# An adaLN block with 32 heads on one core: zero matmuls, GpSimd fills, the table load and the tie-break seeds of a list scheduler

## The chip, the cores and the metric

The kernel runs on 1 core of one Trainium2 chip. The metric is the device time of one execution in microseconds (us). The program is written for five engines with queues of their own: TensorE (PE), VectorE (DVE), ScalarE (ACT), GpSimd (POOL) and SyncE (SP), which issues nearly all DMAs.

## The reference

One transformer block of 2048 rows, width 512, 32 heads of 16, hidden width 1376, in bf16. The vector `c` gives six modulation rows through `w_mod`.

```python
mod = (_silu(c) @ w_mod).reshape(c.shape[0], 6, 1, -1)
sa, ca, ga, sb, cb, gb = (mod[:, 0], mod[:, 1], ..., mod[:, 5])
h = _layernorm(x) * (1 + ca) + sa
x = x + ga * _A_ref(h, A_wqkv, A_wo)                  # softmax attention, 32 heads
h = _layernorm(x) * (1 + cb) + sb
x = x + gb * _B_ref(h, B_w1, B_b1, B_w2, B_b2)        # gelu(h @ w1 + b1) @ w2 + b2
```

## The kernel before, in words

**Tiling.** The 2048 rows are four blocks of 512 (four tiles of 128 each). Attention goes by runs: one run is one query block against all 16 key tiles for four heads, which sit in the four 32-row strips of TensorE. A score unit is one 128 x 512 tile of scores of one head. Two engines take the exponentials from PSUM. ACT takes units two and three at a time and applies Exp (line 1082). DVE takes single units, adds a constant and writes int16, which are read as bf16 powers of two (line 1123); four shifted copies of each such tile (lines 1139, 1155, and on GpSimd 1161), multiplied with values scaled by four weights (the VX tiles, line 961), make the approximation smooth. TensorE computes scores (line 1034), then the products with the values, accumulated in the bank `od` (line 1222).

**The order of work.** Nothing is ordered by hand. At build time a list scheduler, `Plan`, simulates the five engines with a guessed duration for each `Op`. At each step `pick` looks, for each engine, at the operations that could start within a small slack of the first one, and takes the one with the least priority. To this `spread` (line 164) adds up to 0.15, a hash of the planned time (in slices of 12.5 us, each with its own entry of `SEEDS`) and, for operations that aren't PE's, of the line number of the operation's lambda. So the seeds and the line numbers settle ties and near ties. The guessed durations set only the order; on the chip the engines wait on semaphores.

**Keeping TensorE's clock up.** `commit` (line 214) keeps a list of what PE did. If less than HEAT = 1.5 us of array work lies within the last WIN = 3.4 us of planned time, `heat` (line 482) supplies a matmul by the zero tile `warm`: into a free `ax` bank, into the free `od` bank, or, while a run accumulates, as four adds of zero into `od` (`zeros`, line 500). Score products that go to `od` are doubled by zeros in the same way (line 1226).

**One-column sums.** The modulation rows needed as columns, `modB` (sb and cb), are 8 columns of 4 one-column matmuls each (`mod_mm`, line 656). Behind every second column there stands a zero matmul of 384 columns.

**The front.** The first 25 us load x, `w_mod` and the weights, normalise block 0 (`first_norm`) and make its keys, queries and values; exponentials begin, while blocks 1 to 3 are normalised (`parted_norm`; the rows are scaled by `apply`, line 703). GpSimd fills the parts of the value tiles and of the query tiles `qm` that must hold constants (`v_init` 617, `fill` 625, `o_qz` 903). These fills may be planned before 4.6 us or after block 0 is normalised (`early`, line 632; those of `qm` only after). GpSimd also computes the reciprocal root of each norm (`rstd`, line 695). Operations with `port=True` are planned so that DVE's and GpSimd's don't overlap; the fills aren't marked so, the `apply` are. `fits` asks if DVE's next marked operation leaves room; `after_dve` makes a GpSimd instruction wait for the last DVE instruction but one that was issued up to then.

**The end.** Block 3 is handled in two halves. For its last two query tiles the runs are short; `last_tile` (tile 2) and `last_last` (tile 3) project, normalise and run the MLP while the MLP of tiles 0 and 1 (`block_tail` with nt = 2) fills in. Its Gelus wait until all scores are done (`finished`), so ACT loads the Gelu table once, ahead of the first of them in ACT's order. There are two kinds: four pieces for tiles 0 and 1 (line 1476, of which the first is charged 1.3 us for the load), and one over tile 2 (line 1569, charged 1.2 us).

Of the kernel before, what the change touches and what calls it, by code (L numbers as in the profile page):

```python
# [11 lines left out]
ACT = mybir.ActivationFunctionType  # L12
# [38 lines left out]


WIN = 3.4
PEL = 0.24
PEA = 0.38
OVER = 0.0
# [4 lines left out]
AL = 0.055  # L61
FILL = 1.6
SPREAD = 0.15
SEEDS = (118, 698, 446, 86, 892, 273, 31, 57, 754, 651, 382, 787, 223, 128, 602, 744, 188, 333, 922, 439, 126, 575, 750, 516, 486, 576, 568, 332, 464, 494, 369, 909, 695, 214, 876, 486, 865, 254, 984, 347, 648, 207, 351, 794, 757, 475, 181, 40, 889, 834, 265, 449, 537, 182, 641, 600, 63, 147, 391, 720, 850, 728, 549, 401)
HEAT = 1.5
STRETCH = 12.5

# [41 lines left out]
class Plan:  # L109
# [104 lines left out]
    def commit(self, s, o):  # L214
        self.lists[o.eng].remove(o)
        self.now = s
        if o.acq is not None:
            o.slot = min(range(len(o.acq.free)), key=lambda i: o.acq.free[i])
            o.acq.free[o.slot] = 1e18
            o.tile = o.acq.alloc(o.slot)  # L220
        if o.kind == "pv" and s >= self.cool and o.last_left() > 1:
            o.extra, o.us = True, 2 * o.us
        if o.rows is not None:
            o.row = min(o.rows, key=lambda i: self.tiles.get(i, 0.0) if self.mode == "qk" else i)
            o.mode = ("qk", o.row)
        if o.eng == "PE":
            self.done.append((s, o.hot * (o.us if o.mode[0] != "qk" else o.us * (len(o.mode) - 1) / 4)))
            while self.done[0][0] < s - 30.0:
                self.done.popleft()
            tot = 0.0  # L230
            self.fill_at = self.cool = 0.0
            for t, us in reversed(self.done):
                tot += us
                if tot >= HEAT and not self.cool:
                    self.cool = t + WIN
                if tot >= self.fill:
                    self.fill_at = t + WIN
                    break
            if o.mode[0] != self.mode:
                self.mode, self.tiles = o.mode[0], {}  # L240
            for i in o.mode[1:]:
                self.tiles[i] = s + o.us
            self.free["PE"] = s + 0.01
        else:
            self.free[o.eng] = s + o.us
            if o.port:
                self.port[o.eng] = s + o.us
            if o.eng == "DVE" and o.us > 0:
                self.dve = (s, s + o.us, o.port)
# [38 lines left out]
def kernel(  # L288
# [14 lines left out]
    nc = tc.nc  # L303
# [4 lines left out]
    NC = D // P  # L308
# [173 lines left out]
    def heat():  # L482
        if o_warm.end is None or plan.now > plan.until:
            return None
        if min(r_ax.free) <= max(plan.now, plan.cool) and (n_a[0] > 0 or r_od.free[0] > plan.now):
            return Op("PE", lambda o: nc.tensor.matmul(
                out=o.tile, lhsT=warm, rhs=warm[:, 0:1].to_broadcast([P, QB]), start=True, stop=True),
                MM, (o_warm,), lat=PEL, mode=("full", 0), kind="heat", acq=r_ax)
        r = pv_run[0]
        if r is None and r_od.free[0] <= plan.now:  # L490
            return Op("PE", lambda o: nc.tensor.matmul(
                out=o.tile, lhsT=warm, rhs=warm[:, 0:1].to_broadcast([P, QB]), start=True, stop=True),
                MM, (o_warm,), lat=PEL, mode=("full", 0), kind="heat", acq=r_od)
        if r is None or left[r] == 0:
            return None
        return Op("PE", lambda o: zeros(r), MM, (o_warm,), lat=PEL, mode=("pv", 0), kind="heat")

    pv_run = [None]

# [114 lines left out]

    o_v0 = {}

    def v_init(v, w, prio, gate):
        x = v[..., 0:32 * VW].rearrange("p t (h w) -> p t h w", w=VW)
        return [op("POOL", lambda o, to=to, c=c: fill(to, c), 0.2, prio=prio, gate=gate)
                for to, c in ((v[..., 32 * VW:32 * VW + 15], 0.0), (x[:, :, 8:32:8, 0:15], 0.0), (x[..., 16:17], w))]  # L620

    first_ln = [False]
# [1 line left out]

    def fill(to, c):
        got = nc.gpsimd.memset(to, c)
        if first_ln[0] and not filled[0]:
            filled[0] = True
            tc.add_manual_dep(got.ins, z_end[0].ins.name, mybir.DependencyInfo(
                mybir.DependencyClass.Sync, mybir.DependencyReason.DATA), reason="behind the first norm")  # L630

    def early():
        return plan.now < EARLY or first_ln[0]
    o_vx0 = {}
    for b in range(NQ):
        o_v0[b] = v_init(VEB[b], PH_W[0], 1.0 + b, early)
        for t in DKS:
            if t // TPB == b:
                o_vx0[t] = [x for ph in range(1, NPH) for x in v_init(
                    VX[(t, ph)].unsqueeze(1), PH_W[ph], 1.5 + b, early)]  # L640

    o_ce = op("ACT", lambda o: nc.scalar.activation(out=ce, in_=c_bf, func=ACT.Tanh, scale=0.5),
              0.5, (o_c,), prio=0.0)
# [12 lines left out]
    def mod_mm(ps, n, w, m, warmer):  # L656
        col = ps[:, n * NC + m:n * NC + m + 1]
        for j in range(NC):
            nc.tensor.matmul(out=col, lhsT=w[:, j, m * P:(m + 1) * P], rhs=sc[:, j:j + 1],
                             start=(j == 0), stop=(j == NC - 1))  # L660
        if m % 2 and warmer:
            nc.tensor.matmul(out=ps[:, P:QB], lhsT=warm, start=True, stop=True,
                             rhs=warm[:, 0:1].to_broadcast([P, QB - P]))

    def mod_columns(dst, ws, kind, warmer=True):
        mm = chain([(lambda ps, n=n, w=w, m=m: mod_mm(ps, n, w[1](), m, warmer), 0.36 if warmer else 0.22)
                    for n, w in enumerate(ws) for m in range(NC)],
                   [o_sc, o_warm, ws[0][0]], kind, r_ax, [w[2] for w in ws],
                   need=lambda i: ws[i // NC][0], hot=(0.0, 0.45) if warmer else (0.0,))

        def out_(o):
            nc.vector.tensor_copy(out=dst, in_=mm.tile[:, 0:2 * NC])
            nc.vector.tensor_scalar(out=dst[:, NC:2 * NC], in0=dst[:, NC:2 * NC], scalar1=1.0,
                                    scalar2=None, op0=ALU.add)
        return op("DVE", out_, 0.4, (mm,), prio=0.65, rel=(mm,))
# [222 lines left out]
    def make_k(b, cc, kind, acq, eng, after=None):  # L898
# [1 line left out]
        o_k[(cc, b)] = op(eng, lambda o: copy(eng, kT[cc][b], mm.tile[:, 0:QB]), 0.6 if eng == 'DVE' else 0.5, (mm,), prio=0.3,  # L900
                          rel=(mm,))

    o_qz = [op("POOL", lambda o, n=n, p=p: fill(QM[n][:, p, :], 0.0), 0.5, prio=0.5 + n, gate=lambda: first_ln[0])
            for n in range(1, 4) for p in range(2)]

    def make_q(b, cc, kind, acq):
# [519 lines left out]
    def evict_g(g, fs, lo, n, mm, prio=0.3):  # L1426
# [3 lines left out]
            in1=b1c[:, fs[0]:fs[0] + len(fs)].unsqueeze(2).to_broadcast([P, len(fs), n]), op=ALU.add),  # L1430
            0.07 + len(fs) * n * 0.00104, (mm, o_late["b1"]), prio=prio, rel=(mm,))

    def block_tail(b, nt=TPB):
        kind = "tail"
        due(prog() + 15, (TAIL if b < LAST - 1 else TAIL2 if b < LAST else TAIL3) / (9 * nt - 1))
# [39 lines left out]
        if part:  # L1475
            ge = [op("ACT", lambda o, lo=lo, hi=hi: nc.scalar.activation(
                out=g.tile[:, lo:hi, 0:N], in_=g.tile[:, lo:hi, 0:N], func=ACT.Gelu_apprx_tanh),
                0.2 * (hi - lo) * nt / 2 + 0.1 + 1.3 * (lo == 0), ev[lo:hi], lat=0.15, prio=0.5,
                gate=finished) for lo, hi in PARTS]
        else:  # L1480
            ge = [op("ACT", lambda o: nc.scalar.activation(  # L1481
# [58 lines left out]
    def last_tile(r):  # L1540
# [21 lines left out]
        for f0 in range(0, NF, 4):  # L1562
# [5 lines left out]
            ev.append(evict_g(g, fs, t * P, P, mm, 0.02))  # L1568
        ge = op("ACT", lambda o: nc.scalar.activation(  # L1569
            out=g.tile[:, :, t * P:(t + 1) * P], in_=g.tile[:, :, t * P:(t + 1) * P], func=ACT.Gelu_apprx_tanh),  # L1570
            1.2, ev, lat=0.15, prio=0.6, gate=finished)
        w2_part(t, ge, lambda f: ge, x2)

    def last_last(r, t, OT, x2):
# [11 lines left out]
               kind="last", prio=0.2)  # L1586
        st = op("DVE", lambda o: (stats(ln, t, acc.tile), plus_eps(nc.vector, ln, t, t + 1)), 1.0, (w, ln), prio=0.022)
        rs = op("POOL", lambda o: rstd(ln, t, t + 1, True), 0.8, (st,), prio=0.0)
        za = op("DVE", lambda o: apply(ln, z, t, acc.tile), 0.6, (rs, z), prio=0.021, rel=(acc,))
        xa = op("DVE", lambda o: nc.vector.tensor_copy(out=x2.tile[:, t, :], in_=acc.tile), 0.6, (w,), prio=0.2, rel=(acc,))  # L1590
        hd = []
        for e, js in (("DVE", (0, 1)), ("ACT", (2, 3))):
            def tr(o, js=js):
# [182 lines left out]
```

## Time and profile before

| what | value |
|---|---|
| timed runs | median 778.43 us of 3 (778.0 to 778.72) |
| the profiled execution | 777.17 us, span 775.4 us |
| busy share | PE 94%, DVE 94%, ACT 97%, POOL 32% |
| exponentials on ACT, line 1082 | 711.4 us, 626 instructions |
| score tiles on DVE, line 1123 | 314.1 us, 484 instructions |
| first exponential starts | 12.44 us |
| last exponential ends | 756.10 us |
| mean granted clock of TensorE | 0.993 |

The profile is one execution. In its groups, an instruction is named by line, engine, operation and tiles (out<-in), with a count, busy time and mean. An arrow in brackets tells which instruction ended an idle time ahead of it. In the stretches, the busy time of each engine is given with the number of instructions in brackets behind it, and PEclk is the clock that TensorE was granted (1.00 is full).

### The profile page before, as it was taken

How to read it: one execution, taken by the hardware profiler on the slowest of the kernel's cores; microseconds unless marked ns; L12 is line 12 of the kernel's file. 1: busy time of each engine (PE TensorE's matmuls, PEld its weight loads, DVE VectorE, ACT ScalarE, POOL GpSimd, SP SyncE). 2: the span in 40 equal slices, each digit the busy share in tenths (PEclk: the TensorE clock that was granted, in tenths of full speed). 3: DMA queues.
4: the chain of work that ended last, by engine and by line, in shares of the span. 5: the costliest groups of instructions: out<-in, count | busy, mean ns of one | idle time of the engine just before them, and what ended most of it. 6: DMA issues, size and time to landing. Idle time of an engine off the chain costs nothing.

```text
span 775.4 us, 22094 instructions
## 1 busy us (share of the span) xinstructions
PE 728.4 (94%) x8901; PEld 276.3 (36%) x8977; DVE 726.3 (94%) x1302; ACT 750.9 (97%) x675; POOL 248.4 (32%) x477
## 2 busy tenths in 40 slices
PE   8899999999999999999999999999999999999997
PEld 3433332333333222222222223232344434344554
DVE  8889988999999999999999999999899999979983
ACT  5999999999999999999999999999999999999994
POOL 7424531324434441232423233233114342202200
PEclk9999998999999999999999999999999999999999
DMA  7152010000021101000100000000111001100000
GB/s 218 41 168 57 20 42 21 22 17 12 17 74 25 28 22 48 18 9 21 43 19 23 29 24 13 22 20 26 33 53 28 17 19 46 26 22 20 22 4 28
DMA packets 34913, 27.51 MB, mean 35 GB/s; under 512 B 17826, under 2 KB 28675, under 8 KB 34811
## 3 DMA queue, kind: packets, MB, share of 16 engines
q1 hardware_dynamic: 34802, 26.10, 11.9%
q8 instruction: 70, 1.15, 0.6%
q14 instruction: 33, 0.26, 0.1%
q10 hardware_dynamic: 8, 0.00, 0.0%
HBM read 20.50 MB, written 2.59 MB: 30 GB/s over the span
## 4 chain that ended last, share of the span: by engine, by line
ACT 37%; PE 36%; DVE 16%; issue 11%; DMA 0%; DVEq 0%; ACTq 0%
ACT pt L1082 35%; PE od L1222 12%; PE st L1034 10%; DVE ph L1123 6%; DVE sh L1139 5%; PE ax L1399 3%; PE ax L1464 3%; PE ax L1034 2%; PE ax L875 2%; PE ax L946 1%; ACT g L1481 1%; DVE sh L1155 1%; PE ax L1393 1%; DVE ln_s L688 1%; DVE g L1471 1%
## 5 line engine op out<-in xcount | busy, mean ns | idle before, releaser
L1082 ACT ACTIVATE pt<-st 128x1536 bf16<-128x1536 f32 x626 | 711.4, 1313 | 6.4 <-PE st L1034 4.0
L1123 DVE TENSOR_SCALAR ph<-ax 128x512 int16<-128x512 f32 x484 | 314.1, 681 | 16.9 <-PE ax L1034 16.1
L1034 PE MATMUL st<-qm,kT 32*128 32x512 bf16 (+1 forms) x1664 | 246.7, 372 | 20.4 <-ACT pt L1082 14.8
L1139 DVE TENSOR_SCALAR sh<-ph 128x2048 int16<-128x2048 int16 x363 | 239.8, 696 | 3.0 <-PE od L1222 1.6
L1161 POOL TENSOR_TENSOR sh<-ph,pair_sh 128x256 int32<-128x256 int32 x209 | 128.0, 623 | 249.4 <-DVE sh L1139 169.3
L1222 PE MATMUL od<-sh,VX 128*32 128x512 bf16 (+2 forms) x2640 | 168.8, 327 | 3.5 <-DVE sh L1139 2.6
L1034 PE MATMUL ax<-qm,kT 32*128 32x512 bf16 (+1 forms) x512 | 164.6, 367 | 5.4 <-DVE ph L1123 3.9
L1034 PEld LDWEIGHTS <-kT 32*128 32x128 bf16 x2176 | 79.6, 91 | 238.1 <-issue 226.3
L1222 PE MATMUL od<-pt,VEB 128*32 128x512 bf16 (+2 forms) x2156 | 141.5, 324 | 0.2 <-ACT pt L1082 0.2
L1222 PEld LDWEIGHTS <-VX 128*32 128x32 bf16 x2640 | 61.1, 95 | 83.8 <-issue 72.6
L1222 PEld LDWEIGHTS <-VEB 128*32 128x32 bf16 x2816 | 65.4, 96 | 66.5 <-issue 52.1
L1291 POOL TENSOR_TENSOR OT<-OD,RB 128x256 bf16<-128x256 f32 x36 | 26.3, 741 | 84.4 <-DVE sh L1139 29.5
L1155 DVE TENSOR_SCALAR sh<-ph 128x2048 int16<-128x2048 int16 (+3 forms) x89 | 50.8, 578 | 1.1 <-PE od L1222 1.1
L1222 PE MATMUL od<-ph,VEB 128*32 128x512 bf16 (+2 forms) x660 | 48.8, 327 | 0.8 <-DVE OD L1264 0.7
L1464 PE MATMUL ax<-blk,W 128*128 128x512 bf16 (+1 forms) x153 | 40.9, 351 | 2.1 <-issue 1.1
L961 POOL TENSOR_SCALAR VX<-VEB 128x128 bf16<-128x128 bf16 x64 | 24.3, 380 | 37.4 <-DVE VEB L720 34.3
L1291 POOL TENSOR_TENSOR OS<-OD,RB 128x256 bf16<-128x256 f32 x24 | 17.2, 729 | 57.6 <-DVE sh L1139 29.3
L1399 PE MATMUL ax<-w,g 128*128 128x512 bf16 x108 | 30.2, 381 | 2.9 <-ACT g L1569 1.3
L875 PE MATMUL ax<-blk,w 128*128 128x512 bf16 x85 | 29.1, 391 | 2.0 <-issue 0.9
L699 POOL TENSOR_TENSOR rs<-rs,mhalf 128x2 f32<-128x2 f32 (+2 forms) x17 | 13.0, 762 | 40.9 <-DVE rs L693 40.0
L1471 DVE TENSOR_SCALAR g<-ax,b1c 128x512 bf16<-128x512 f32 x33 | 24.3, 742 | 0.5 <-PE ax L1464 0.4
L1399 PEld LDWEIGHTS <-g 128*128 128x128 bf16 x187 | 15.4, 97 | 24.1 <-issue 12.3
(133 smaller groups left out, 426.0 us busy)
## 6 DMA issues: line engine op xcount, KB each, us to landing
RB<-rn SPq DMA_DIRECT2D x120, 64.0 KB
xb<-in_A_x_dram SPq DMA_DIRECT2D x7, 512.0 KB
qm<-qs SPq DMA_DIRECT2D x120, 16.0 KB
out_dram<-o SPq DMA_DIRECT2D x15, 128.0 KB
W<-in_B_w_dram SPq DMA_DIRECT2D x1, 1376.0 KB
w<-in_A_wqkv_dram SPq DMA_DIRECT2D x3, 384.0 KB
g<-in_w_mod_dram SPq DMA_DIRECT2D x4, 256.0 KB
g<-in_w_mod_dram SPq DMA_DIRECT2D x2, 512.0 KB
```

Of the source, the lines that this page charges most:

```text
L875: return chain([(lambda ps, j=j: nc.tensor.matmul(out=ps[:, 0:QB], lhsT=w.tile[:, j, cc * P:(cc + 1) * P], rhs=o_h[b].tile[:, j, :], start ...
L1034: nc.tensor.matmul(out=o.tile[:, k * QB + n * w:k * QB + (n + 1) * w], lhsT=kT[cc][kb][rows, ko * P:(ko + 1) * P], rhs=qm.tile[rows, par, ...
L1082: nc.scalar.activation(out=e.tile[:, 0:len(got) * QB], in_=o.tile[:, 0:len(got) * QB], func=ACT.Exp, scale=ESC)
L1123: nc.vector.tensor_scalar(out=ph.tile[:, o.row * QB:(o.row + 1) * QB], in0=o.tile, scalar1=PH_B, scalar2=0.0, op0=ALU.add, op1=ALU.max)
L1139: sh = op("DVE", lambda o, j=j: nc.vector.tensor_scalar(out=o.tile, in0=first.tile, scalar1=PH_SH[j], scalar2=None, op0=ALU.add), 0.6, es, ...
L1155: return nc.vector.tensor_scalar(out=sh.tile[:, at], in0=first.tile[:, at], scalar1=PH_SH[-1], scalar2=None, op0=ALU.add)
L1161: return nc.gpsimd.tensor_tensor(out=sh.tile[:, at].bitcast(I32), in0=first.tile[:, at].bitcast(I32), in1=pair_sh[:, 0:1].to_broadcast([P, ...
L1222: nc.tensor.matmul(out=o_od[r].tile[32 * i:32 * i + 32, to:to + w], lhsT=v_tile(k, ph)[:, c0:c0 + 32], rhs=got[i][:, n * w:(n + 1) * w], s ...
L1291: two = beside(lambda c: nc.gpsimd.tensor_tensor(out=both_heads(OT.tile, tile_of[r]) if r in tile_of else OT.tile[:, c], in0=OD.tile[:, c] ...
L1399: nc.tensor.matmul(out=ps, lhsT=g[:, f, col:col + P], rhs=rhs[:, c], start=(f == 0), stop=(f == NF - 1))
L1464: mm = chain([(lambda ps, f=f, j=j, f0=f0: nc.tensor.matmul(out=ps[:, (f - f0) * N:(f - f0 + 1) * N], lhsT=W1[:, j, f * P:(f + 1) * P], rh ...
L1471: ev += [op("DVE", lambda o, f=f, f0=f0, mm=mm: nc.vector.tensor_scalar(out=g.tile[:, f, 0:N], in0=mm.tile[:, (f - f0) * N:(f - f0 + 1) * ...
```

## The change

Seven things, all in the code that makes the order or in single operations:

1. In the first 30 us of planned time, the window in which 1.5 us of array work must lie is 2.4 us, not 3.4.
2. `heat` prefers the adds of zero into `od` whenever a run accumulates; before, a free `ax` bank came first.
3. A zero matmul stands behind every one-column sum, not behind every second.
4. GpSimd's fills are marked `port`, with longer durations; after the first norm they are planned only where `fits` finds room, and each but the first waits for the DVE instruction before the last. Those of `qm` may also go before 4.6 us.
5. The load of the Gelu table is an ACT operation in the plan, without an instruction, ahead of both kinds of Gelu, whose durations are changed.
6. In `last_last`, the copy of the projected tile goes from DVE to ACT; the norm is planned behind it.
7. Nine of the 64 seeds differ, and the lines shift by 1 to 5.

```diff
+WIN_EARLY = 2.4
...
-SEEDS = (118, 698, ..., 651, 382, ..., 602, 744, 188, ..., 794, ..., 889, ..., 147, 391, 720, ...)
+SEEDS = (948, 698, ..., 651, 812, ..., 502, 744, 928, ..., 821, ..., 825, ..., 428, 944, 328, ...)
...
-            tot = 0.0
+            tot, win = 0.0, WIN if s > 30.0 else WIN_EARLY
...
-                    self.cool = t + WIN
+                    self.cool = t + win
...
-                    self.fill_at = t + WIN
+                    self.fill_at = t + win
...
     def heat():
         if o_warm.end is None or plan.now > plan.until:
             return None
+        if pv_run[0] is not None and left[pv_run[0]] > 0:
+            return Op("PE", lambda o, r=pv_run[0]: zeros(r), MM, (o_warm,), lat=PEL, mode=("pv", 0), kind="heat")
...
-        if r is None or left[r] == 0:
-            return None
-        return Op("PE", lambda o: zeros(r), MM, (o_warm,), lat=PEL, mode=("pv", 0), kind="heat")
+        return None
...
-    def v_init(v, w, prio, gate):
+    def v_init(v, w, prio, gate, us=0.25):
...
-        return [op("POOL", lambda o, to=to, c=c: fill(to, c), 0.2, prio=prio, gate=gate)
+        return [op("POOL", lambda o, to=to, c=c: fill(to, c), us, prio=prio, gate=gate, port=True)
...
-        if first_ln[0] and not filled[0]:
+        if first_ln[0] and filled[0]:
+            after_dve(got)
+        elif first_ln[0]:
...
-        return plan.now < EARLY or first_ln[0]
+        return plan.now < EARLY or first_ln[0] and plan.fits(0.3)
...
-                    VX[(t, ph)].unsqueeze(1), PH_W[ph], 1.5 + b, early)]
+                    VX[(t, ph)].unsqueeze(1), PH_W[ph], 1.5 + b, early, 0.13)]
...
-        if m % 2 and warmer:
+        if warmer:
...
-        mm = chain([(..., 0.36 if warmer else 0.22)
+        mm = chain([(..., 0.38 if warmer else 0.22)
...
-                   need=lambda i: ws[i // NC][0], hot=(0.0, 0.45) if warmer else (0.0,))
+                   need=lambda i: ws[i // NC][0], hot=(0.42,) if warmer else (0.0,))
...
-    o_qz = [op("POOL", ..., 0.5, prio=0.5 + n, gate=lambda: first_ln[0])
+    o_qz = [op("POOL", ..., 0.53, prio=0.5 + n, gate=early, port=True)
...
+    o_table = op("ACT", None, 1.3, (), lat=0.0, prio=-1.0, gate=finished)
...
-                0.2 * (hi - lo) * nt / 2 + 0.1 + 1.3 * (lo == 0), ev[lo:hi], lat=0.15, prio=0.5,
+                0.23 * (hi - lo) * nt / 2 + 0.05, ev[lo:hi] + [o_table], lat=0.15, prio=0.5,
...
-            1.2, ev, lat=0.15, prio=0.6, gate=finished)
+            1.4, ev + [o_table], lat=0.15, prio=0.6, gate=finished)
...
-        za = op("DVE", lambda o: apply(ln, z, t, acc.tile), 0.6, (rs, z), prio=0.021, rel=(acc,))
-        xa = op("DVE", lambda o: nc.vector.tensor_copy(out=x2.tile[:, t, :], in_=acc.tile), 0.6, (w,), prio=0.2, rel=(acc,))
+        xa = op("ACT", lambda o: nc.scalar.copy(out=x2.tile[:, t, :], in_=acc.tile), 0.62, (st,), prio=0.2, rel=(acc,))
+        za = op("DVE", lambda o: apply(ln, z, t, acc.tile), 0.6, (rs, z, xa), prio=0.021, rel=(acc,))
```

More of the change, by code (lines that the diff above doesn't have):

```diff
@@ L63 @@
 SPREAD = 0.15
-SEEDS = (118, 698, 446, 86, 892, 273, 31, 57, 754, 651, 382, 787, 223, 128, 602, 744, 188, 333, 922, 439, 126, 575, 750, 516, 486, 576, 568, 332, 464, 494, 369, 909, 695, 214, 876, 486, 865, 254, 984, 347, 648, 207, 351, 794, 757, 475, 181, 40, 889, 834, 265, 449, 537, 182, 641, 600, 63, 147, 391, 720, 850, 728, 549, 401)
+SEEDS = (948, 698, 446, 86, 892, 273, 31, 57, 754, 651, 812, 787, 223, 128, 502, 744, 928, 333, 922, 439, 126, 575, 750, 516, 486, 576, 568, 332, 464, 494, 369, 909, 695, 214, 876, 486, 865, 254, 984, 347, 648, 207, 351, 821, 757, 475, 181, 40, 825, 834, 265, 449, 537, 182, 641, 600, 63, 428, 944, 328, 850, 728, 549, 401)
 HEAT = 1.5
@@ L665, in mod_columns @@
     def mod_columns(dst, ws, kind, warmer=True):
-        mm = chain([(lambda ps, n=n, w=w, m=m: mod_mm(ps, n, w[1](), m, warmer), 0.36 if warmer else 0.22)
+        mm = chain([(lambda ps, n=n, w=w, m=m: mod_mm(ps, n, w[1](), m, warmer), 0.38 if warmer else 0.22)
                     for n, w in enumerate(ws) for m in range(NC)],
                    [o_sc, o_warm, ws[0][0]], kind, r_ax, [w[2] for w in ws],
-                   need=lambda i: ws[i // NC][0], hot=(0.0, 0.45) if warmer else (0.0,))
+                   need=lambda i: ws[i // NC][0], hot=(0.42,) if warmer else (0.0,))
         def out_(o):
@@ L901, in make_k @@
                           rel=(mm,))
-    o_qz = [op("POOL", lambda o, n=n, p=p: fill(QM[n][:, p, :], 0.0), 0.5, prio=0.5 + n, gate=lambda: first_ln[0])
+    o_qz = [op("POOL", lambda o, n=n, p=p: fill(QM[n][:, p, :], 0.0), 0.53, prio=0.5 + n, gate=early, port=True)
             for n in range(1, 4) for p in range(2)]
```

## The prediction

> **What bounds it now.** I read the engine table first: ScalarE (ACT) is 97% busy and 711.4 of its 750.9 us are the exponentials of line 1082. VectorE (DVE) and TensorE (PE) are both at 94%. All three matter, because planner lines 389 to 421 hand score tiles to ACT and to DVE as each comes free. The work has (34-2) x 16 x 4 = 2048 score units (TOTAL, line 979). Row L1123 shows DVE taking 484 of them, so ACT takes 1564. ACT needs 711.4/1564 = 0.455 us a unit. DVE needs (314.1+239.8+50.8)/484 = 1.25 us a unit. Together they finish 2.20 + 0.80 = 3.0 units a us. So a us of ACT idleness costs 0.73 us of the whole, and a us of DVE idleness 0.27 us. I use these two prices everywhere before the end.
>
> Next I read the busy table by stretches, to see where ACT and DVE are short. Columns: stretch, its length, busy us of PE, PE's weight loads, DVE, ACT, GpSimd (POOL), the granted clock, DMA share, GB/s.
>
> ```profile
> 12.44:25.20 12.76, 10.08 (x92) 4.72 (x93) 12.45 (x31) 10.77 (x13) 9.08 (x46) 0.87 0.45 146
> 25.20:116.00 90.80, 84.73 (x896) 32.56 (x900) 81.93 (x159) 90.75 (x87) 37.49 (x69) 1.00 0.23 63
> 116.00:122.80 6.80, 6.80 (x61) 2.02 (x61) 4.65 (x9) 5.56 (x5) 0.00 (x0) 0.50 0.04 7
> 122.80:756.12 633.32, 601.69 (x7660) 223.11 (x7723) 611.01 (x1062) 630.23 (x546) 192.38 (x318) 1.00 0.10 26
> 756.12:758.84 2.72, 1.30 (x16) 0.52 (x17) 1.52 (x4) 2.71 (x3) 0.00 (x0) 1.00 0.00 0
> 758.84:771.81 12.97, 12.87 (x104) 8.10 (x105) 5.09 (x12) 6.43 (x17) 0.55 (x1) 1.00 0.10 32
> ```
>
> The middle is full: between 122.8 and 756.1 ACT is idle 3.1 us in all. What is loose lies in three places: 2 us of ACT before 25.2, 1.2 us in a stretch that ran wholly at half clock, and a PE that is half idle from 756.12 and then full to 771.81.
>
> Last I asked what PE did ahead of the two half-clock stretches. The clock's edges (17.01, 20.42, 116.00, 122.82) lie on one grid of 3.41 us, so I took one grid window ahead of each fall, grouped by shape.
>
> ```profile
> L1034 PE MATMUL st<-qm,kT 32*128 32x512 bf16 x10 | 1.8, 445 | 0.9 <-ACT pt L1082 0.8
> L1034 PE MATMUL ax<-qm,kT 32*128 32x512 bf16 x4 | 1.5, 381 | 0.0
> L1222 PE MATMUL od<-pt,VEB 128*32 128x512 bf16 x8 | 0.8, 391 | 0.0
> L659 PE MATMUL ax<-sc,g 128*128 128x1 bf16 x12 | 0.6, 166 | 0.0
> L662 PE MATMUL ax<-warm 128*128 128x384 bf16 x1 | 0.3, 322 | 0.0
> ```
>
> Eight 512-column matmuls in a row at 761.66 take 1.89 us, of which the last is 0.38, so one steps every 0.216 us. One on 32 rows or 32 columns uses a quarter of the array: I weigh it 0.054. So the window 112.58 to 116.00 holds (10+4+8) x 0.054 + 0.16 = 1.35 us, 39% of it; the twelve one-column sums add next to nothing although each shows 166 ns of busy. The window 13.60 to 17.01 holds 8 score matmuls and 11 full ones of 128 columns, 8 x 0.054 + 11 x 0.054 = 1.03 us, 30%. I did the same for all 227 windows: these two are the lowest of all that ran at full clock before the end, and the next (34.08) holds 41% and kept its clock. So the fall comes somewhere between 39% and 41%.
>
> **The change part by part.**
>
> *A zero matmul behind every one-column sum (line 661).* Four more of 384 columns, 0.16 us each (0.322 us as the row shows a single one with its latency). In the window 112.58 to 116.00 the sums m = 0 and m = 2 also ran, so the new window would hold 1.35 + 2 x 0.16 = 1.67 us or 49%, above the 41% that kept the clock. If the fall goes, ACT gets back its waits between 116 and 124 (0.8 on st and 0.7 on ax by the view of waits): 1.5 x 0.73 = 1.1 us. DVE's waits there for score tiles are 3.1 us: 0.84 us more. Bounds 0 and 1.9. I take **-1.5**, since DVE also waited 3.7 us just before, at full clock. The four matmuls cost PE 0.64 us; PE shares its time with ACT's bound only where it is late, so I put **+0.1**.
>
> *WIN_EARLY and zeros first in heat (lines 231 to 237, 482 to 496), GpSimd's zeros kept off VectorE's norms (lines 617 to 633, 903).* These meet in the front. The rows:
>
> ```profile
> 14.46 1.88 DVE L705 TENSOR_SCALAR z<-xb,mv,rs 128x512 bf16<-128x512 bf16 x2
> 14.47 1.29 POOL L626 MEMSET qm<- 128x512 bf16 x2
> 17.48 1.45 ACT L1082 ACTIVATE pt<-st 128x1536 bf16<-128x1536 f32 x1 [0.41 <-PE st L1034]
> 19.84 1.02 ACT L1082 ACTIVATE pt<-st 128x1024 bf16<-128x1024 f32 x1 [0.91 <-PE st L1034]
> ```
>
> One norm took 1562 ns, where the median of its line is 406: it ran beside a zero fill of qm. That 1.16 us delays the transposes of block 1, its modulate and its keys, which ACT then waits for; and PE, starved meanwhile, loses its clock from 17.01 to 20.42, where ACT is busy 2.09 of 3.41 us. ACT's waits from 12 to 25 are 2.1 us in all: 2.1 x 0.73 + 1.16 x 0.27 = 1.85 us if everything goes, 0 if DVE, busy 12.45 of 12.76 us, is late anyway. A zero matmul on the way of a ready one costs up to 0.39 us. I take **-1.0**.
>
> Each fill after the first norm now also waits for the DVE instruction before the last one issued. Behind the fills in POOL's queue stand the reciprocal roots (L699) of the next norms and the VX scalings (L961). One such wait is in the trace (0.7 us, qm L626 behind z L705); most others would find their instruction done, because POOL trails. I cost them at nothing, from the cover that the VX tiles are first used at 46.3 us. The qm fills that may now go into POOL's first 4.6 us take the place of others there, at nothing.
>
> *The table load a step of its own (o_table), new estimates for the Gelus.* The load is in the kernel already; only the planner's order moves. The end, as it is:
>
> ```profile
> 756.12 1.28 ACT L1569 ACT_TABLE_LOAD   x1
> 757.41 1.38 ACT L1569 ACTIVATE g<-g 128x1408 bf16<-128x1408 bf16 x1
> 758.70 2.81 ACT L1476 ACTIVATE g<-g 128x512 bf16<-128x512 bf16 x4
> 758.84 1.04 PE L1399 MATMUL ax<-w,g 128*128 128x512 bf16 x4 [1.34 <-ACT g L1569]
> 759.72 0.59 PE L1526 MATMUL t<-WoP,OT 128*128 128x512 bf16 x2
> ```
>
> PE waits 1.34 us for the long Gelu, because the planner put the load on another one, and from then on PE is full (12.87 of 12.97 us). The order of the two kinds is settled by priority plus the hash of line and seed (`spread`). Worked out by hand for the time slices round the end, it gave the long Gelu 0.617 against 0.645 before; with the new lines and seeds the short ones have 0.51 to 0.61 and the long one 0.67 to 0.74. So the short ones go first, the first of them takes 0.61 us (its row's minimum), and PE starts at 757.40 + 0.61 + 0.06 (the step from the long Gelu's end to PE's start) = 758.07 instead of 758.84. What PE must do afterwards is the same. Bounds 0 and 1.34; I take **-0.7**.
>
> *The copy of the last tile from DVE to ACT (L1590, 0.68 us).* DVE's norm at 762.63 comes sooner, but PE is full there, so nothing comes of it; ACT is idle 2.5 us ahead of its next step at 763.99, which hides the copy. Without that cover it costs 0.6 us. **0**.
>
> *Nine seeds, and every line number, changed.* Each tie on DVE, ACT and POOL falls anew from start to end. The sign is open; from the 3.1 us that ACT idles in the middle and what one half-clock stretch cost, I bound it by 1.5 us either way. **0**.
>
> Sum: -1.5 + 0.1 - 1.0 - 0.7 = -3.1 us. The profiled execution took 777.17 us (span 775.4 and 1.77 around it), which would become 774.1. The median of the timed runs is 778.43, 1.26 us above it, so I forecast **775.3 us**.
>
> **A rule that speaks against it.** The Trainium skill, "TensorE: Matmul & The Clock Gate", section "Part 1: The HAM clock gate", says that the clock is halved after at least one idle window of about 3.4 us. The trace agrees with the length of the window (3.41 us). It does not agree on idleness: PE shows as busy 2.63 of 3.42 us ahead of the fall at 116.00. By that rule more zeros would change nothing; that is the first rival below.
>
> **The rivals.**
>
> *The clock falls as before* (chance 0.16). If something other than array activity decides, or if the chain of sums is issued later than now, both half-clock stretches stay. Against it: the two lowest windows of 227 are exactly the two that fall. Left are -0.7 at the end and about -0.6 of the front, for the norm: 777.1 us.
>
> *New falls elsewhere* (0.12). The new order can push other windows under 40%; five that kept their clock lie at 41 to 46% (34.08, 740.63, 136.48, 40.90, 529.01). Two new ones at 1.5 us each give 778.3 us.
>
> *GpSimd's queue becomes the bound of the front* (0.15, the slower side). Between 8.81 and 24.65 POOL is busy 14.6 of 15.85 us, 11.3 of it 52 fills: it has 1.25 us to spare. If one fill in six is held by the 0.67 us that the one existing wait shows, the roots behind them slip 9 x 0.67 = 6 us; norms, keys and with them ACT and DVE slip as much. That is +6.0 against -1.5, -0.7 and +0.1: 782.3 us. Four held fills eat the rest of the gain. Against it: POOL trails DVE there, so its fences are mostly met.
>
> *The new order also fills DVE's holes* (0.07): DVE idles 8.9 us between 25.2 and 116. All of it is worth 8.9 x 0.27 = 2.4: 772.9 us.
>
> **Numbers.** Forecast 0.50, spread from 773.4 to 777 by the bounds above. The resolution is 0.2%, 1.56 us, so faster begins below 776.9. Faster: 0.50 + 0.07 + some of the first rival's spread, 0.62. Same: 0.22. Slower: 0.16. The range for 8 in 10 is 772.2 to 779.6: it leaves out most of the POOL rival and the ends of the reordering.
>
> **What would show it.** Right: full clock from 112 to 125 and from 13 to 21 us; every norm L705 of the front near 0.4 us; ACT's waits before 25 us under 1 us; a Gelu of 512 or 768 elements right behind the table load and PE starting within 0.8 us of the load's end. Wrong: a half-clock stretch in either place, fills and L699 after 25 us with ACT waiting for keys, or new half-clock stretches in the middle.

## The result and the profile after

The changed kernel takes 775.69 us (median of 7 runs, 774.42 to 778.23), the kernel before 778.43 us (7 runs, 778.0 to 779.32). The ratio is 0.9966, 95% interval 0.9952 to 0.9979: faster by 2.7 us, or 0.34%. The forecast was 775.3. The total came out; of the parts that made it, most did not, as the profile shows at once. The profiled execution took 775.04 us, with a span of 773.3.

The busy table of the changed kernel by the same stretches (the last three are set to its own end):

```profile
12.44:25.20 12.76, 10.58 (x82) 4.54 (x83) 10.11 (x29) 8.89 (x9) 7.79 (x29) 0.73 0.48 158
25.20:116.00 90.80, 84.87 (x913) 33.43 (x920) 81.64 (x159) 90.72 (x89) 32.10 (x76) 1.00 0.23 64
116.00:122.80 6.80, 6.11 (x72) 2.14 (x68) 6.58 (x15) 6.80 (x8) 4.27 (x7) 1.00 0.03 6
122.80:754.19 631.39, 603.51 (x7682) 224.44 (x7744) 613.84 (x1062) 629.09 (x544) 201.99 (x334) 1.00 0.10 26
754.19:756.86 2.67, 2.62 (x112) 2.00 (x102) 2.16 (x5) 2.65 (x4) 0.00 (x0) 1.00 0.02 6
756.86:769.66 12.80, 12.75 (x105) 8.11 (x104) 5.47 (x13) 6.94 (x17) 0.55 (x1) 1.00 0.10 32
```

Three things are to be seen. From 116.0 to 122.8 the clock is full and ACT is never idle: that loss is gone, as forecast. From 12.4 to 25.2 things became worse: the granted clock fell from 0.87 to 0.73 and ACT is busy 8.89 us, not 10.77. And at the end PE no longer waits, yet it is full up to 769.66, and from the last exponential to the end of the span it is 19.1 us, where it was 19.3. The MLP's first product comes 2.67 us after the table load begins (754.19 to 756.86), before 2.72: PE fills the time with the last products of attention instead.

The front, line by line:

```profile
13.92 1.05 POOL L627 MEMSET VEB<- 128x60 bf16 x3 [0.49 <-DVE mv L692]
14.56 0.74 POOL L627 MEMSET VX<- 128x15 bf16 x3
15.16 0.71 POOL L702 TENSOR_TENSOR rs<-rs,mhalf 128x2 f32<-128x2 f32 x1
15.90 0.73 DVE L708 TENSOR_SCALAR z<-xb,mv,rs 128x512 bf16<-128x512 bf16 x2 [0.69 <-POOL rs L702]
18.63 1.45 ACT L1085 ACTIVATE pt<-st 128x1536 bf16<-128x1536 f32 x1 [1.53 <-PE st L1037]
```

The two norms take 0.73 us together (before 1.88), so keeping the fills off them worked. But they start at 15.90, before at 14.46. Two things delay them. DVE's statistics of block 1 start 0.66 us later (12.16, not 11.50) because they wait for a block of x from the DMA; b_front below, with the old fills, shows that wait too (12.14), so it isn't the change's. And the root of line 702 now stands behind two groups of fenced fills: it starts 1.26 us after its input is begun (line 696, at 13.90), where before it was 0.33 us, and DVE waits 0.69 us for it. ACT then waits 1.53 us. Its waits from 12 to 25 us are 4.0 us in all, before 2.1.

What TensorE did in the grid window ahead of the fall, 12.715 to 16.128, grouped by shape:

```profile
L949 PE MATMUL ax<-w,blk 128*128 128x128 bf16 x16 | 1.1, 220 | 0.0
L1037 PE MATMUL st<-qm,kT 32*128 32x512 bf16 x5 | 0.8, 379 | 0.7 <-ACT pt L1085 0.7
L887 PE MATMUL ax<-blk,w 128*128 128x256 bf16 x1 | 0.3, 283 | 0.0
```

By the weights of the prediction that is 16 x 0.054 + 5 x 0.054 + 0.107 = 1.24 us, 36%: too little again by the prediction's measure, with no zero matmul in it at all. The clock was halved from 16.13 to 22.96, two grid windows where before had one.

### The profile page after: what moved, and what is told of

Same layout as the page of the kernel before. It is cut to its first block, busy times and chain, and to the rows that moved or that the text cites. A ratio compares the mean times of both kernels' runs of the same rounds, so it can differ in the third digit from the quotient of the medians.

```text
span 773.3 us, 22319 instructions
## 1 busy us (share of the span) xinstructions
PE 731.4 (95%) x9020; PEld 279.7 (36%) x9096; DVE 728.9 (94%) x1304; ACT 749.6 (97%) x674; POOL 255.7 (33%) x494
## 4 chain that ended last, share of the span: by engine, by line
PE 38%; DVE 29%; ACT 21%; issue 7%; DMA 2%; SPq 1%; POOL 0%; DVEq 0%; ACTq 0%; POOLq 0%
ACT pt L1085 21%; PE od L1225 14%; DVE ph L1126 13%; PE st L1037 10%; DVE sh L1142 8%; PE ax L1402 3%; PE ax L1037 3%; PE ax L878 2%; DVE sh L1158 2%; PE ax L1469 2%; DVE g L1476 1%; DVE ln_s L691 1%; DVE OD L1267 1%; DMA dc<-dn 1%; DVE xb L1451 1%
## 5 line engine op out<-in xcount | busy, mean ns | idle before, releaser
L1142 DVE TENSOR_SCALAR sh<-ph 128x2048 int16<-128x2048 int16 x366 | 243.8, 699 | 1.1 <-PE od L1225 0.5
L1164 POOL TENSOR_TENSOR sh<-ph,pair_sh 128x256 int32<-128x256 int32 x226 | 136.0, 611 | 277.9 <-DVE sh L1142 172.4
L1225 PE MATMUL od<-sh,VX 128*32 128x512 bf16 (+2 forms) x2704 | 171.5, 324 | 3.2 <-DVE sh L1142 2.2
L1037 PEld LDWEIGHTS <-kT 32*128 32x128 bf16 x2176 | 81.4, 91 | 225.7 <-issue 213.1
L1225 PEld LDWEIGHTS <-VX 128*32 128x32 bf16 x2704 | 62.8, 95 | 83.1 <-issue 71.8
L1158 DVE TENSOR_SCALAR sh<-ph 128x2048 int16<-128x2048 int16 (+3 forms) x85 | 48.6, 579 | 3.3 <-PE od L1225 3.0
L878 PE MATMUL ax<-blk,w 128*128 128x512 bf16 x87 | 29.2, 393 | 2.0 <-issue 0.6
L691 DVE BATCH_NORM_STATS2 ln_s<-xb 128x6 f32<-128x512 bf16 x31 | 21.1, 679 | 2.0 <-DMA xb<-in_A_x_dram 1.9
```

The source lines that it names most:

```text
L878: return chain([(lambda ps, j=j: nc.tensor.matmul(out=ps[:, 0:QB], lhsT=w.tile[:, j, cc * P:(cc + 1) * P], rhs=o_h[b].tile[:, j, :], start ...
L1037: nc.tensor.matmul(out=o.tile[:, k * QB + n * w:k * QB + (n + 1) * w], lhsT=kT[cc][kb][rows, ko * P:(ko + 1) * P], rhs=qm.tile[rows, par, ...
L1142: sh = op("DVE", lambda o, j=j: nc.vector.tensor_scalar(out=o.tile, in0=first.tile, scalar1=PH_SH[j], scalar2=None, op0=ALU.add), 0.6, es, ...
L1158: return nc.vector.tensor_scalar(out=sh.tile[:, at], in0=first.tile[:, at], scalar1=PH_SH[-1], scalar2=None, op0=ALU.add)
L1164: return nc.gpsimd.tensor_tensor(out=sh.tile[:, at].bitcast(I32), in0=first.tile[:, at].bitcast(I32), in1=pair_sh[:, 0:1].to_broadcast([P, ...
L1225: nc.tensor.matmul(out=o_od[r].tile[32 * i:32 * i + 32, to:to + w], lhsT=v_tile(k, ph)[:, c0:c0 + 32], rhs=got[i][:, n * w:(n + 1) * w], s ...
```

## The experiments

The edits of matmuls and fills keep the planner's order as it was ("order held"): a matmul is issued inside an operation that the plan already has, with its planned duration unchanged, so every engine's instructions follow as before but for the few that are added, moved or taken out. In f_fills_old GpSimd's fills are planned anew, and two zeros before 9 us change places. The two seed runs draw the whole order anew, and the two runs of the end change it there. That matters, since anything that the planner sees draws all ties anew.

Each run also has its mean granted clock c, from which the number of half-clock windows follows as (1 - c) x 2 x span / 3.413 us (c has three digits, so the count is good to about a quarter of a window). The grid of the clock stands differently in every run: its first edge lies anywhere from 4.0 to 6.8 us after the first instruction in the 14 traces. So a weak stretch costs a window in some runs and none in others. The kernel before ran 71 times beside the experiments. In 70 of these runs the count goes from 0.5 to 7, with a median of 3.2, and the time rises by 1.20 us a window from 774.8 (correlation 0.95). The other one shows a clock of 0.939, some 28 windows, and took 784.29 us, 0.34 us a window. So 1.20 us is a price for the places where this kernel's clock usually falls, not for any window. The changed kernel's seven runs: 774.42 with one window, a median of 775.69 with two (five runs), 778.23 with four.

| kernel | median us (runs) | ratio to before, 95% interval | median at 0 windows (runs) |
|---|---|---|---|
| b_sums | 777.19 (12) | 0.9971 (0.9950 to 0.9991) | 775.21 (1) |
| b_front | 778.12 (12) | 0.9990 (0.9974 to 1.0007) | none |
| b_both | 776.07 (9) | 0.9942 (0.9924 to 0.9961) | 775.46 (4) |
| b_tail | 775.64 (12) | 0.9945 (0.9928 to 0.9963) | 775.06 (6) |
| b_seeds_new | 792.07 (5) | 1.0165 (1.0145 to 1.0186) | 790.73 (1) |
| a_sums_odd | 776.57 (12) | 0.9967 (0.9948 to 0.9985) | 773.79 (1) |
| a_front | 773.48 (6) | 0.9933 (0.9911 to 0.9955) | 773.36 (4) |
| f_fills_old | 773.80 (6) | 0.9926 (0.9897 to 0.9955) | 773.59 (3) |
| f_nofence | 773.40 (6) | 0.9933 (0.9916 to 0.9950) | 773.05 (2) |
| f_tail_old | 773.34 (6) | 0.9933 (0.9914 to 0.9952) | 772.62 (4) |
| f_spots | 775.49 (12) | 0.9961 (0.9946 to 0.9977) | 774.92 (5) |
| f_seeds_old | 784.81 (11) | 1.0071 (1.0046 to 1.0097) | 783.84 (3) |

b_ stands on the kernel before, a_ on the changed one, f_ on the changed one with the front zeros of a_front. The kernel before measured 778.43, 780.37 (b_both, b_tail, f_fills_old, f_seeds_old) and 778.82 us (f_spots, f_nofence, f_tail_old, b_seeds_new) beside them. Its median count of windows was 3.2, 5.0 and 3.2 there, and that moves the ratios too. So neither medians nor ratios compare cleanly across the three groups; the last column does it best, and rests on few runs.

**b_sums: the sums' zeros alone.**

```diff
-        if m % 2 and warmer:
+        if warmer:
```

> The kernel before, with a zero matmul of 384 columns behind all eight one-column sums; the planner's durations are left as they were, so every engine's order is the same. Theory A (array activity in a window of 3.41 us decides, and the fall at 116 us costs about 1.2 us for each of its two half-clock windows): the window ahead of the fall goes from 39% to about 49%, the half-clock stretch from 116.0 to 122.8 us is gone, the time is 1.5 to 2.5 us below before (776.0 to 776.9). Rival (zeros change nothing, as no window is idle): the stretch stays, 778.4.

The half-clock stretch at 116 us is gone; ACT is busy throughout it:

```profile
116.00:122.80 6.80, 6.32 (x84) 2.44 (x84) 5.64 (x12) 6.80 (x7) 0.00 (x0) 1.00 0.04 7
```

The grid stands elsewhere in this run, so one profile doesn't settle it; the counts do. Beside it 20 of 29 runs of the kernel before had three windows or more, and none of the 12 of b_sums had. In the stretch 112.58 to 116.00 the work by the prediction's weights is now 19 x 0.054 + 3 x 0.16 + 0.216 = 1.72 us, 50%. The time fell by 1.2 us between the medians and by 0.29%, 2.3 us, by the ratio; the median lies 0.3 us above the expected range. One edit of four small matmuls, with nothing else changed, takes the fall away although no window there was idle. The rival is out for this place.

**a_sums_odd: the changed kernel without them.** The edit is the reverse.

> The changed kernel with the zero matmul behind odd columns only, order held. Theory A: in the new order the adds of zero into od already keep the windows round the sums at 55% or more, and four matmuls of 384 columns spread over 10 us take at most 5 to 10 points off one window, so the clock stays full there and the time stays within 0.5 us of the changed kernel (775.2 to 776.2). Rival (the four extra matmuls are what keeps the clock): one or two half-clock windows near 120 us, 1.2 to 2.5 us slower (777 to 778).

```profile
116.00:122.80 6.80, 6.08 (x77) 2.30 (x73) 6.80 (x15) 6.80 (x7) 3.53 (x6) 1.00 0.04 7
```

The clock stays full without them too, and the median count of windows is 1.8, as in the changed kernel, not one or two more. So it isn't the extra four that hold the clock in the changed kernel. In the new order, adds of zero into `od` stand there already (line 503 has 28 matmuls between 105 and 124 us, line 502 before had 8). In these runs either cure is enough. That nothing at all is lost isn't shown: the ratio, 0.9967, is the changed kernel's 0.9966, but the median, 776.57, is 0.9 us above it and outside the expected range. By luck the profiled run also shows the front without a fall (its grid had a window from 14.91, already at 45%) and a span of 772.0.

**b_front and a_front: zeros in the front.** Six zero matmuls (five in b_front) ahead of the first transposes of block 1, which wait for the norm:

```diff
                 def tr(o, part=part, js=js):
+                    if (b, part) == (1, 0):
+                        for _ in range(6):
+                            nc.tensor.matmul(out=o.tile, lhsT=warm, rhs=warm[:, 0:1].to_broadcast([P, QB]), start=True, stop=True)
                     for n, j in enumerate(js):
```

(In the kernels this stands within the loop's line, so that no line moves.)

> The changed kernel with six more zero matmuls of 512 columns issued ahead of the first transposes of block 1, where TensorE waits 1.1 us for the norm at about 15.2 us; order held otherwise. Theory A: the windows from 12.7 to 16.1 and 16.1 to 19.5 us rise from 36% to 50% and more, the 6.8 us at half clock are gone, ACT's waits before 25 us fall from 4.0 to about 2 us, and the time falls by 1.5 to 2.5 us (773.2 to 774.2), with less spread from run to run. Rival B (the front is late because of the norm, the roots on GpSimd and the DMA, and the clock only follows): the clock is full and the time is within 0.5 us of the changed kernel.

> The kernel before with five more zero matmuls of 512 columns ahead of the first transposes of block 1, order held. Theory A: the half-clock window from 17.0 to 20.4 us is gone and the time falls by about 1.2 us (777.2). Rival B: the norm that lasts 1.56 us sets the front, the clock is full there but the time is within 0.5 us of before (778.0 to 778.9).

The same rows of a_front:

```profile
12.44:25.20 12.76, 10.76 (x109) 5.30 (x106) 11.05 (x32) 10.39 (x11) 8.17 (x31) 1.00 0.52 161
15.23 1.48 PE L853 MATMUL ax<-warm 128*128 128x512 bf16 x6
15.71 0.73 DVE L708 TENSOR_SCALAR z<-xb,mv,rs 128x512 bf16<-128x512 bf16 x2 [0.70 <-POOL rs L702]
```

The clock is full, ACT's waits fall from 4.0 to 2.5 us, and the time from 775.69 to 773.48; four of six runs have no half-clock window. In the kernel before, the same cure leaves 778.12, ratio 0.9990 with 1 inside its interval. The same stretch of b_front:

```profile
12.44:25.20 12.76, 9.82 (x96) 4.91 (x96) 12.32 (x33) 10.77 (x12) 9.41 (x46) 1.00 0.51 162
```

The clock is full, yet ACT is busy 10.77 us, to the digit what it was at 0.87, and waits 2.1 us as before; the first two norms still take 1.50 us. So in the kernel before the front's half-clock window costs ACT nothing that can be seen, and rival B holds there; with two such windows, as in the changed kernel, the clock counts. (In b_front's profile x also came 0.64 us later, so the comparison isn't clean.) The fall at the sums, which this edit leaves, came at 116.9 in that profile and lasted four windows (13.65 us). The median count went from 3.2 to 2.3, and the time didn't follow.

**b_both: both cures in the kernel before.** The two edits together, with six zeros.

> The kernel before with both cures in its held order: a zero matmul behind every one-column sum and six zeros of 512 columns ahead of block 1's first transposes. Theory A: no half-clock window is left before the last microseconds, and the time is what the runs of before extrapolate to at none, about 775.4 us; what then remains to the changed kernel with the front zeros (773.48) is no matter of the clock but of order: about 1.9 us. Rival: the clock was all there was, and this kernel comes to 773.5 us as well.

Without half-clock windows it takes 775.46, and a_front takes 773.36. f_fills_old, which ran beside b_both, takes 773.59 there, so the gap isn't one between groups of runs. The clock wasn't all: about 2 us of the difference are a matter of order. (The line through the runs of before gives 774.8 at none, which would leave 1.4.) Not every window is gone, as the expectation had it: five of the nine runs still have one, in the profile at 263.8 us.

**b_tail: the end alone.** On b_both, with the table load's line in the place of an empty one, and 0.75 as the long Gelu's priority, which puts the short ones first (the change left it at 0.6):

```diff
+    o_table = op("ACT", None, 1.3, (), lat=0.0, prio=-1.0, gate=finished)
-                0.2 * (hi - lo) * nt / 2 + 0.1 + 1.3 * (lo == 0), ev[lo:hi], lat=0.15, prio=0.5,
+                0.23 * (hi - lo) * nt / 2 + 0.05, ev[lo:hi] + [o_table], lat=0.15, prio=0.5,
-            1.2, ev, lat=0.15, prio=0.6, gate=finished)
+            1.4, ev + [o_table], lat=0.15, prio=0.75, gate=finished)
```

> The kernel before with both cures, and in its end alone the plan's table load as a step of its own and the short Gelus first; order held until the last exponential. Prediction's step: TensorE starts on the MLP's second half 0.77 us sooner and the time is 0.7 us below the kernel with both cures (about 774.7 if that is 775.4). Rival: TensorE has as much to do and is full to the end, what it gains at the start it loses in waiting for the long Gelu or in the norm's chain: within 0.2 us of the kernel with both cures.

```profile
755.30 1.28 ACT L1476 ACT_TABLE_LOAD   x1
756.60 2.83 ACT L1476 ACTIVATE g<-g 128x512 bf16<-128x512 bf16 x4
757.28 0.39 PE L1399 MATMUL ax<-w,g 128*128 128x512 bf16 x1 [0.59 <-ACT g L1476]
757.51 0.59 PE L1526 MATMUL t<-WoP,OT 128*128 128x512 bf16 x2
...
769.32 0.81 PE L1399 MATMUL ax<-W2c,g 128*128 128x512 bf16 x3
770.52 0.69 DVE L1535 TENSOR_TENSOR o<-ax,xb 128x512 bf16<-128x512 f32 x1 [1.85 <-DMA out_dram<-o]
```

PE's first product comes 1.98 us after the start of the load, where b_both has 2.72: 0.74 sooner, against the 0.77 of the prediction. But the last sum of the kernel, PE being done at 770.13, starts at 770.52: it waits for the DMA that empties its output tile (there are two). From the load to the end of the span it is 18.76 us, in b_both 19.25: 0.5 us of the 0.74 are left. The median at 0 windows is 0.4 us lower; the ratios' intervals overlap, so in the timed runs the gain isn't clear of noise.

**f_tail_old: the end as before, in the new order.** Parts 5 and 6 of the change are undone.

> The changed kernel with the front zeros and the end planned as before: no table load in the plan, the old durations of the Gelus, the copy of the last tile on DVE. The order is the same up to the last exponentials, and the short Gelus stay first, since the long one's inputs come late in this order. Prediction's step (-0.7 us at the end from the load's step): slower by 0.4 to 0.7 us. Rival (in the changed order the Gelus stand as they should anyway): within 0.2 us of 773.5.

773.34, against 773.48: nothing. From the load to the end it is 19.18 us, in a_front 19.08. In the new order the long Gelu's inputs come late (the last part of its matrix product runs at 755.7 in the changed kernel), so the short ones go first whatever the plan thinks of the load.

**f_fills_old and f_nofence: GpSimd's fills.** The first undoes all of part 4 of the change; the second only the waits:

```diff
         if first_ln[0] and filled[0]:
-            after_dve(got)
+            pass
```

> The changed kernel with the front zeros, and GpSimd's fills planned as before (not kept off DVE's norms, no waits on DVE, those of qm only after the first norm); the other engines' orders are the same but for two swaps of zeros before 9 us. Prediction's step (the fills' place is worth the 1.16 us that the norm lost): a norm L708 of about 1.5 us comes back near 15 us, and the time is 0.5 to 1.0 us above 773.5. Rival (the waits put on the fills cost the roots what the norm gains): the roots come about 0.8 us sooner, the norm is longer, and the time is within 0.4 us of 773.5.

> The changed kernel with the front zeros, without the waits of GpSimd's fills on DVE, all orders held. If the waits hold up the roots in the front (0.5 and 0.65 us of waits ahead of fills, and DVE waiting 0.7 us for a root): the first root of block 1 comes 0.4 to 0.9 us sooner and the time falls by up to 0.6 us. If the waits keep the norms short: a norm of over 0.6 us appears before 25 us and the time stays within 0.3 us of 773.5.

773.80 and 773.40: neither is told from 773.48. The root of block 1 in f_nofence:

```profile
15.18 0.71 POOL L702 TENSOR_TENSOR rs<-rs,mhalf 128x2 f32<-128x2 f32 x1 [0.62 <-DVE rs L696]
```

Without the waits the root starts 0.25 us after its input is begun (line 696, at 14.93), with the old fills 0.50 us, in a_front 1.27 us. (The clock times themselves don't compare: x landed later in f_nofence, whose statistics start at 13.20, in a_front at 11.96.) So the waits hold the root up by some 0.8 to 1.0 us in these profiles; the late x of f_nofence, for which GpSimd idles 0.62 us, may flatter it. The norms lengthen in return: the longest takes 0.69 us in f_nofence and 0.93 in f_fills_old, in the changed kernel 0.51. The time shows neither. That the one gives back what the other gains fits this, but isn't shown; both may be too small to see.

**f_seeds_old and b_seeds_new: the seeds crossed over.** One line each: the changed code with the old seeds, and the old code with the new ones. These are drawn anew.

> The changed kernel with the front zeros and the seeds of before, so that ties fall anew in nine slices and all that follows them. Theory A with order as the rest: the 1.9 us that are not the clock's come from the seeds and lines as a draw, so another draw gives anything from 772.5 to 776.5, most likely slower than 773.5 by about 1 us. Rival (the rest comes from the edits themselves): within 0.5 us of 773.5.

> The kernel before with both cures and the seeds of the changed kernel on its own lines. Theory A (seeds fit only the lines and durations that they were drawn for; the old seeds on the changed kernel cost 11 us): 5 to 12 us slower than the kernel with both cures at 775.5, so 780 to 788. Rival (the new seeds are better in themselves): 773 to 775.

+11.3 us on a_front and +16.0 on b_both by the medians, 10.7 and 17.4 by the ratios. Both expectations had less. Neither list is better in itself: each is worse on the other's lines and durations. Where the time goes in f_seeds_old is read from the rows of DVE's and GpSimd's score work, a_front first:

```profile
L1126 DVE TENSOR_SCALAR ph<-ax 128x512 int16<-128x512 f32 x488 | 316.0, 680 | 12.9 <-PE ax L1037 11.7
L1164 POOL TENSOR_TENSOR sh<-ph,pair_sh 128x256 int32<-128x256 int32 x226 | 136.2, 612 | 278.3 <-DVE sh L1142 172.4 <-DVE ph L1126 57.6 <-PE od L1225 11.1
```

and f_seeds_old:

```profile
L1126 DVE TENSOR_SCALAR ph<-ax 128x512 int16<-128x512 f32 x480 | 313.3, 682 | 18.6 <-PE ax L1037 17.1
L1164 POOL TENSOR_TENSOR sh<-ph,pair_sh 128x256 int32<-128x256 int32 x196 | 118.5, 613 | 299.5 <-DVE sh L1142 207.8 <-DVE ph L1126 37.4 <-DVE OD L1267 11.4
```

DVE takes 8 units fewer and waits 5.4 us more for score banks, GpSimd 30 shift pieces fewer. The exponentials end 5.9 us later (the table load starts at 758.31, not 752.42), and the end after it lasts 22.4 us, not 19.1. In b_seeds_new it goes another way: DVE takes 484 units, as in b_both, the load starts 6.3 us later (762.10, not 755.84), and the end lasts 29.2 us, not 19.3, with ACT waiting 7.6 us for one product. So a draw can cost time in the middle, at the end, or both.

**f_spots: zeros at two changes of run.** In a_front's trace, the sliding share of array work still falls to 36-38% near 291 and 611 us.

```diff
-            if o.extra:
+            if o.extra or r in (11, 25) and left[r] in (1, 2):
                 zeros(r)
```

> The changed kernel with the front zeros, and four adds of zero into od more, ahead of two changes of run (near 291 and 611 us) where the sliding share of array work still falls to 36-38%; order held. Theory A: no window of any phase of the grid lies under 40% before the end, so every execution runs without a half-clock window; the median falls by 0.2 to 0.4 us against the kernel with the front zeros alone (773.1 to 773.4) and the spread shrinks. Rival: the adds stand in the way of the last products of the run, 0.2 to 0.5 us slower.

775.49: slower by some 2 us than its sisters, at equal counts of windows too (774.92 at none). Theory A fails on the windows as well: seven of the 12 runs still have one or two. In the profile the clock falls at 44.35, a place that the edit leaves alone; f_nofence's falls at 43.93 and f_fills_old's at 45.56. That the adds stand in the way, as the rival said, is likely, but its 0.5 us are not enough: 16 matmuls of a quarter of the array step 16 x 0.054 = 0.86 us. ACT waits 1.1 us more on `ax` (2.0 against 0.9). Where the rest goes is open.

## Why the prediction was right or wrong

**The sums' zeros, -1.5 +0.1.** The place, the mechanism and roughly the size hold: on the kernel before, alone, they gave -1.2 us by the medians and -2.3 by the ratio. (DVE's 3.1 us of waits run to 125 us; up to 124 they are 2.7.) What fails is whose merit it is: the changed kernel keeps its clock there without them.

**The front, -1.0.** Wrong in sign wherever the clock falls there. The norm shrank as said, and the term went on from there as though ACT's 2.1 us of waits would go with the norm and the clock. They don't: in the nine traces whose front ran at full clock ACT waits 1.4 to 2.9 us for scores, with short norms and with long ones, and none is under the 1 us that I named as a sign of being right. In the changed kernel the clock is the larger part: with zeros put in and nothing else, 2.2 us come back (a_front). The smaller window WIN_EARLY put no matmul into the gap; I take it that on the planner's clock the norm isn't late there, which no run shows. And the cost that I set at nothing, the fences' on GpSimd's queue, is there: the root comes some 0.8 to 1.0 us later behind its input, with 0.69 us of DVE waiting. That was the slower rival, with a slip of 1 us at most, not 6. The rival also had too little room for GpSimd: 14.6 us is a sum of rows that overlap in time, and by engine POOL is busy 12.53 of the 15.84 us from 8.81 on, which leaves 3.3 us, not 1.25. In the time the slip can't be seen.

**The end, -0.7.** The mechanism holds in the old order, with 0.74 of 0.77 us at PE's start and 0.5 us of the end in the trace; the output tile takes some back. In the new order it gives nothing: the sign that PE starts on the MLP within 0.8 us of the load's end failed (1.39 us, 755.47 to 756.86). The term was worked out on an order that the change itself replaced.

**The seeds and lines, 0 with 1.5 us either way.** This is the step that was wrong by most. I bounded a new draw by the idle time that was left, as though a draw could only shift small waits. It also shifts how many tiles DVE and GpSimd can take and how long the end lasts, and the runs show draws of +11 and +16 us. With the old seeds on its own lines the changed kernel would be slower than the kernel before (784.81 even with the front cured), so its gain hangs on nine seeds that fit.

**The sum.** Measured -2.7, forecast -3.1. By the counts of windows, 3.2 down to 1.8 at 1.2 us each, the clock gives -1.7: the sums' stretch gained more than that and the front lost some of it. The remaining 1.0, or 1.4 to 2.1 by the runs without half-clock windows, is order. So the total was right by luck: its parts were off by more than the total, and cancelled. What in the order gives it (the preference for zeros into `od`, the durations or the draw of ties) wasn't told apart, because each of these is itself a new draw.

**The threshold.** I put the fall between 39% and 41% of a window. Counted that way, with each matmul that touches the window taken whole, the windows ahead of a fall held 30 to 44% over the 14 traces, and some from 37% up led to none. So the two neat numbers of one trace were an accident. Most of that band is counting at the edges. If each matmul counts by the part of it that lies inside the window, and one is put in for each weight load whose matmul has no record (some 75 in ten of the traces), the 12 windows ahead of a fall held 23 to 37%, and the 3107 at full clock that led to none held 36% or more. The busy share doesn't part them. Two windows of b_front, which lacks no record:

```profile
113.49:116.91 3.42, 2.64 (x41) 1.42 (x40) 3.35 (x10) 3.42 (x5) 0.00 (x0) 1.00 0.01 2
758.61:762.02 3.41, 1.90 (x52) 0.89 (x44) 1.52 (x4) 3.38 (x5) 0.00 (x0) 1.00 0.00 0
```

PE is busy 77% of the first, which holds 33% of a full window's work and led to a fall, and 56% of the second, which holds 43% and led to none. The rule of an idle window, from the Trainium skill ("TensorE: Matmul & The Clock Gate", "Part 1: The HAM clock gate"), isn't what these runs show: b_sums moved the share of one stretch from 39% to 50% and the fall was gone.

**A better kernel.** a_front is below both: 773.48, ratio 0.9933 to before (0.9911 to 0.9955); its interval and the changed kernel's (from 0.9952) just overlap, and three variants of it (f_fills_old, f_nofence, f_tail_old) lie at the same 773.3 to 773.8.

## What to carry to other kernels

Weigh TensorE's work by rows, columns and length over each stretch of 3.4 us, sliding, not by its busy share: in these traces a stretch under about 37% cost its clock when the grid fell on it, and a few zero matmuls placed in an existing wait cured it without touching the order. In the way of ready work they cost more than they gave (f_spots), and a cured clock need not give time: b_front's gave none that can be seen. Where a list scheduler breaks ties by a hash, every edit is a new draw, and here a bad draw cost four to six times what the whole change gave: test edits with the order held, and never price a reordering by the idle time it finds. A gain worked out on the old order of a stage counts only if that order survives the change.

## What the runs showed of the hardware that was not expected

The granted clock's grid of 3.413 us runs free of the kernel: the same kernel had 0.5 to 7 half-clock windows in 70 runs, and that goes with most of its spread (1.2 us a window, correlation 0.95). By the finer count above, half-clock windows that held 31 to 38% of a full-speed window's work were followed by another, and those at 40 to 47% ended the stretch. So about the same amount of work ends a half-clock stretch as prevents one.
